# Scores and the second GEMM as 64-row tiles of TensorE in an attention-and-GEMM kernel

## Chip, cores, metric

One core of one Trainium2 chip. The metric is the device time of one execution in microseconds (us), the median of several runs. The engines are named as the profile names them: PE (TensorE matmuls), PEld (its weight loads), DVE (VectorE), ACT (ScalarE), POOL (GpSimd), SP (SyncE, which here only issues transfers).

## The reference, cut to what matters

```python
# q, k, v: (8 batches, 8 heads, 576 tokens, 64); f: (8, 8, 576)
scores = matmul(q, k.T) / 8
scores = where(causal, -1e9, scores + cumsum(log f)[q] - cumsum(log f)[k])
attn   = softmax(scores)
x      = matmul(attn, v)               # -> 4608 tokens x 512
out    = gelu(x @ w_in) @ w_out        # 512 -> 2048 -> 512
```

The kernel works in bf16 with fp32 sums. It folds the forget term into v, so that scores are a bare q k product, then an exponential, a causal mask and AV.

## The kernel before

Batches run one after the other. While batch b is in attention, TensorE fills the gaps of ScalarE's exponentials with the **second GEMM of batch b-1**, one matmul of 128 x 512 a step, 64 steps a batch. Then follows the first GEMM of batch b: 16 tiles of 4 matmuls, each drained by a gelu.

A pair of heads (i, four a batch) has its k transposed in one tile kT of 128 rows: head 0 in rows 0 to 63, head 1 in rows 64 to 127. The contraction of a head is only 64 rows long. The kernel before keeps two copies of q, each with the other head's half zeroed, and runs 128-row matmuls:

```python
qA = [consts.tile([P, S], BF16, ...)]   # head 0 in rows 0-63, zeros below
qB = [consts.tile([P, S], BF16, ...)]   # head 1 in rows 64-127, zeros above

def scores(b, i, t):                    # one of four score tiles of a pair
    on_pe = b == 0 or (b == 1 and i == 0)
    st = s_psum.tile([P, 2, 512], FP32, tag="s")       # two banks; two buffers
    for n, q0, w in STILES[t]:
        for h, qt in enumerate((qA[i], qB[i])):
            nc.tensor.matmul(st[:, h, c : c + w],
                kT[i][:, K0[n] : K0[n] + P], qt[:, q0 : q0 + w], ...)
        if on_pe ...:                   # causal mask, added by TensorE in the first batches
            nc.tensor.matmul(st[:, h, c : c + P], ident_bf, after, start=False, ...)
    nc.scalar.activation(et[:, :, 0:c], st[:, :, 0:c], Act.Exp, scale=scale)
    ...                                 # later batches: mask by GpSimd
```

The second GEMM uses one PSUM bank a block of 128 tokens (16 steps), and one copy to take it out. The same pool `m_psum` (two banks) also serves the first GEMM.

```python
def gemm2(c, ...):                      # a generator: one step a yield
    for ts, kt, ... in order:
        if kt == 0:
            pss[ts] = m_psum.tile([P, d_model], FP32, tag="m")
        nc.tensor.matmul(pss[ts], g_of[c][kt][:, ts * P : (ts + 1) * P],
                         w_out_sb[:, kt, :], start=kt == 0, stop=kt == n_ff - 1)
        if kt == n_ff - 1:
            nc.vector.tensor_copy(ot, pss[ts]); nc.sync.dma_start(out[...], ot)
        yield

FILL = [[4, 6, 2, 2], [2, 2, 2, 2], [2, 2, 2, 2], [2, 2, 1, 1], [8, 0, 20]]
# attention(b): for each pair i and tile t: scores(b, i, t);
#   AV of pair i-1 in parts behind tiles 1, 2 and 3; then FILL[i][t] steps
# last pair: AV, then x by a transposing DMA under 20 more steps (PE transposes for b <= 2)
```

The pools hold eight PSUM banks (PSUM is where this kernel's matmuls write their sums; a bank is counted here as a tile of 128 x 512 fp32): scores 2 x 2, AV (`o_psum`) 2, `m_psum` 2. The change keeps to these eight, so a second bank for a block comes out of one of the three pools.

The softmax here doesn't subtract the row's maximum and nothing guards it: scores larger than these inputs give would overflow.

## Time and profile before

| | before |
|---|---|
| median of the runs | 357.1 us |
| TensorE busy | 346.8 of 356.2 us |
| from the last first-GEMM matmul of one batch to that of the next: batch 1, 2, 3 to 7 | 40.81, 38.14, 37.42 us |

The third row is taken from the trace's single records; the parts before batch 1 vary from run to run by up to a few us; the first GEMM of batch 0 begins at 28.75 here, and the clock record reaches full at 10.7 here. Three rows of the list of groups show the terms (line, engine, operation, out<-in, shapes, count; then busy us and mean ns; then idle time ahead of them and what ended it):

```profile
L308 PE MATMUL s<-qA,kT 128*128 128x256 bf16 (+2 forms) x192 | 51.9, 282 | 2.1 <-ACT e L323 2.0
L323 ACT ACTIVATE e<-s 128x896 bf16<-128x896 f32 (+1 forms) x128 | 105.1, 863 | 19.8 <-PE s L308 11.3
L451 DVE COPY ot<-ps 128x512 f32<-128x512 f32 (+2 forms) x37 | 25.1, 677 | 105.3 <-PE ps L442 105.0
```

Before the score matmuls of this row TensorE stood idle for 2.1 us in the whole span, 2.0 of them for ScalarE, so the schedule has next to no gap. ScalarE needs 0.86 us to drain a scores tile, VectorE 0.68 to take out a block. "128*128" is the part of the array that a matmul uses: this is where a tile of 64 rows will show as 64*128.

### The profile page before, as it was taken

Reading aid. Unit: us, or ns where it says so; the run is one execution under the profiler, and the core shown is the slowest. Engines: PE = TensorE matmul, PEld = TensorE weight load, DVE = VectorE, ACT = ScalarE, POOL = GpSimd, SP = SyncE. Lnnn points to the kernel's source line nnn. Section 1 sums busy time; section 2 is a strip of 40 time slices with the busy share of each in tenths; the row PEclk is TensorE's granted clock in tenths of the full one; section 3 lists DMA queues with packets and bytes.
Section 4 is the critical chain, followed back from the end, with each engine's and each line's share of the span. In section 5 each row is a group of like instructions: output and inputs, shape, how many; then the busy total and the mean of one; then the engine's idle time right before and its main releaser. Section 6 shows DMA issues by size and latency. Waiting matters only on the chain.

```text
span 356.2 us, 7069 instructions
## 1 busy us (share of the span) xinstructions
PE 346.8 (97%) x2756; PEld 190.7 (54%) x2756; DVE 182.1 (51%) x482; ACT 217.4 (61%) x298; POOL 124.5 (35%) x243
## 2 busy tenths in 40 slices
PE   8998989999999999999999999999999999999995
PEld 3784556544664466445654565446544664444443
DVE  6771984595467625781559145924584361011011
ACT  5697586368854797279826882688457854603600
POOL 7390275406546044804470256215520530000000
PEclk9999999999999999999999999999999999999999
DMA  7999999885997894489639973979310132011013
GB/s 116 169 188 191 190 155 202 183 192 90 205 158 161 146 185 122 95 142 189 144 98 134 188 139 82 174 141 173 76 66 2 45 61 81 2 59 59 2 30 88
DMA packets 103936, 43.85 MB, mean 123 GB/s; under 512 B 82720, under 2 KB 99360, under 8 KB 103904
## 3 DMA queue, kind: packets, MB, share of 16 engines
q1 hardware_dynamic: 86608, 29.26, 40.4%
q0 software_dynamic: 16896, 13.63, 25.6%
q10 hardware_dynamic: 400, 0.52, 0.4%
q8 instruction: 21, 0.34, 0.4%
q14 instruction: 11, 0.09, 0.1%
HBM read 36.85 MB, written 9.44 MB: 130 GB/s over the span
## 4 chain that ended last, share of the span: by engine, by line
PE 94%; ACT 2%; DMA 1%; issue 1%; DVE 1%; POOL 0%; ACTq 0%; DVEq 0%; POOLq 0%
PE ps L404 35%; PE ps L442 35%; PE s L308 13%; PE o L344 8%; ACT e L323 2%; PE ps_f L198 1%; DMA k<-in_k_dram 1%; PE s L317 1%; PE ps_w L187 1%; PE ps_x L380 0%; PE s_t L233 0%; PE ps_t L233 0%; DVE x L360 0%; ACT xt L368 0%; ACT g L416 0%
## 5 line engine op out<-in xcount | busy, mean ns | idle before, releaser
L416 ACT ACTIVATE g<-ps 128x512 bf16<-128x512 f32 x144 | 86.0, 597 | 97.9 <-PE ps L404 97.8
L442 PE MATMUL ps<-w_out_sb,g 128*128 128x512 bf16 (+2 forms) x592 | 143.8, 373 | 0.0
L323 ACT ACTIVATE e<-s 128x896 bf16<-128x896 f32 (+1 forms) x128 | 105.1, 863 | 19.8 <-PE s L308 11.3
L404 PE MATMUL ps<-xT,w_in_sb 128*128 128x512 bf16 x512 | 112.9, 379 | 0.7 <-ACT xT L383 0.6
L325 POOL TENSOR_SCALAR_AFFINE_SELECT e<-e 128x256 bf16<-128x256 bf16 x135 | 53.7, 408 | 118.6 <-ACT e L323 117.7
L404 PEld LDWEIGHTS <-w_in_sb 128*128 128x128 bf16 x576 | 56.0, 97 | 69.2 <-issue 3.9
L451 DVE COPY ot<-ps 128x512 f32<-128x512 f32 (+2 forms) x37 | 25.1, 677 | 105.3 <-PE ps L442 105.0
L442 PEld LDWEIGHTS <-g 128*128 128x128 bf16 x592 | 52.2, 98 | 41.8
L292 POOL TENSOR_TENSOR vw<-v_sb,wT 128x640 bf16<-128x640 f32 x32 | 41.0, 1282 | 45.7 <-PE ps_t L233 15.9
L308 PEld LDWEIGHTS <-kT 128*128 128x128 bf16 x384 | 36.7, 98 | 33.3 <-issue 6.2
L308 PE MATMUL s<-qA,kT 128*128 128x256 bf16 (+2 forms) x192 | 51.9, 282 | 2.1 <-ACT e L323 2.0
L308 PE MATMUL s<-qB,kT 128*128 128x256 bf16 (+2 forms) x192 | 48.6, 282 | 0.0
L344 PE MATMUL o<-vw,e 128*128 128x65 bf16 x960 | 43.5, 194 | 0.5 <-ACT e L323 0.4
L344 PEld LDWEIGHTS <-e 128*128 128x128 bf16 x960 | 39.5, 98 | 7.5 <-ACT e L323 0.5
L359 DVE RECIPROCAL r<-o 128x5 f32<-128x5 f32 x64 | 12.5, 195 | 41.5 <-PE o L344 41.0
L276 DVE COPY kT<-tk 64x288 bf16<-64x288 bf16 x96 | 32.3, 336 | 1.4
L360 DVE TENSOR_TENSOR x<-o,r 128x256 bf16<-128x256 f32 x64 | 27.2, 425 | 2.4 <-DVE r L359 0.2
L276 DVE COPY qB<-tq 64x288 bf16<-64x288 bf16 x48 | 18.8, 391 | 0.6
L370 DVE TENSOR_SCALAR xt<-o,r 64x64 bf16<-64x64 f32 x60 | 17.5, 291 | 1.4
L276 DVE COPY qA<-tq 64x288 bf16<-64x288 bf16 x48 | 17.1, 355 | 1.1
L404 PE MATMUL ps<-tails,w_in_sb 128*128 128x512 bf16 x64 | 14.4, 377 | 0.0
L416 ACT ACT_TABLE_LOAD x8 | 10.3, 1283 | 0.1
(63 smaller groups left out, 124.4 us busy)
## 6 DMA issues: line engine op xcount, KB each, us to landing
out_dram<-ot SPq DMA_DIRECT2D x32, 256.0 KB, 2.2
v_sb<-in_v_dram SPq DMA_DIRECT2D x20, 256.0 KB, 4.7
v_sb<-in_v_dram SPq DMA_DIRECT2D x29, 128.0 KB, 5.4
q<-in_q_dram POOLq DMA_DIRECT2D x6, 576.0 KB, 6.6
k<-in_k_dram POOLq DMA_DIRECT2D x6, 576.0 KB, 9.0
w_in_sb<-in_moe_w_in_dram POOLq DMA_DIRECT2D x4, 512.0 KB, 7.6
w_out_sb<-in_moe_w_out_dram POOLq DMA_DIRECT2D x4, 512.0 KB, 9.6
q<-in_q_dram POOLq DMA_DIRECT2D x4, 144.0 KB, 4.1
```

The costliest lines, as they stand in the source:

```text
L276: nc.vector.tensor_copy(rows[:, odd], src[odd * D : (odd + 1) * D, 2 * i + h].rearrange("d j p -> d p j"),)
L292: nc.gpsimd.tensor_tensor(vw_of[b][:, hs, :, 0:D], v_sb[:, hs, :, :], w.unsqueeze(3).to_broadcast([P, 2, NBLK, D]), Alu.mult,)
L308: nc.tensor.matmul(st[:, h, c : c + w], kT[i][:, K0[n] : K0[n] + P], qt[:, q0 : q0 + w], start=True, stop=not on_pe or c not in SDIAG[t],)
L323: nc.scalar.activation(et[:, :, 0:c], st[:, :, 0:c], Act.Exp, scale=scale)
L325: nc.gpsimd.affine_select(out=et[:, :, c0 : c0 + P], in_=et[:, :, c0 : c0 + P], compare_op=Alu.is_ge, fill=0.0, base=0, pattern=[[0, 2], [ ...
L344: nc.tensor.matmul(o[:, m, :], e_of[b, i, t][:, h, c : c + P], vw_of[b][:, 2 * i + h, n, :], start=(n == 0), stop=(n == m),)
L360: nc.vector.tensor_tensor(x_of[b, i][:, :, h, :], o[:, 0:4, 0:D], r[:, 0:4].unsqueeze(2).to_broadcast([P, NBLK - 1, D]), Alu.mult,)
L370: nc.vector.tensor_scalar(*tail, r[D:P, 4:5], None, Alu.mult)
L404: nc.tensor.matmul(ps, w_in_sb[:, kt, ffb * P : (ffb + 1) * P], src[:, kt, :], start=(kt == 0), stop=(kt == n_dm - 1),)
L416: nc.scalar.activation(g_of[c][ffb], ps, Act.Gelu)
L442: nc.tensor.matmul(pss[ts][:, c0:c1], g_of[c][kt][:, ts * P : (ts + 1) * P], w_out_sb[:, kt, c0:c1], start=(kt == 0), stop=(kt == n_ff - 1),)
L451: nc.vector.tensor_copy(ot[:, c0:c1], pss[ts][:, c0:c1])
```

## The change

Its intent: run the two heads' score matmuls at the same time as two tiles of 64 rows, with no zeros (qT replaces qA and qB). A change between tilings takes 0.09 us in the trace of the kernel before (from 13.06 to 13.15, between 128*128 and 96*64), so the second GEMM's steps that stand among the scores are made of 64-row tiles too: each step is two half contractions into two banks, added on the way out by a copy and an add. AV stays at 128 rows, so it moves into one stretch a pair, with some whole steps ("n") between its two heads.

```diff
-            for h, qt in enumerate((qA[i], qB[i])):
+            for h in range(2):
+                d = slice(h * D, (h + 1) * D)
                 nc.tensor.matmul(
                     st[:, h, c : c + w],
-                    kT[i][:, K0[n] : K0[n] + P],
-                    qt[:, q0 : q0 + w],
+                    kT[i][d, K0[n] : K0[n] + P],
+                    qT[i][d, q0 : q0 + w],
...
+    STEPS = [16 * "r", "rrrnnrrrrrrrrnnn", "rrrrrrrrrrnnrrrr", 8 * "r" + 8 * "n"]
+    def gemm2_rows(c):
+        for ts, steps in enumerate(STEPS):
+            if ts < n_sub - 1:
+                banks = [m_psum.tile([P, d_model], FP32, tag="m", name="ps2")
+                         for _ in range(2)]
+            else:
+                both = s_psum.tile([P, 2, d_model], FP32, tag="s", name="ps2")
+                banks = [both[:, 0], both[:, 1]]
+            for kt, step in enumerate(steps):
+                last = kt == steps.rindex("r")
+                for r in range(2 if step == "r" else 1):
+                    rows = slice(r * D, (r + 1) * D) if step == "r" else slice(0, P)
+                    nc.tensor.matmul(banks[r], g_of[c][kt][rows, ...],
+                                     w_out_sb[rows, kt, :], ...)
+                if last:
+                    nc.vector.tensor_copy(ot, banks[1])
+                if kt == n_ff - 1:
+                    nc.vector.tensor_tensor(ot, ot, banks[0], Alu.add)
...
-    FILL = [[4, 6, 2, 2], [2, 2, 2, 2], [2, 2, 2, 2], [2, 2, 1, 1], [8, 0, 20]]
+    FILL = [[6, 6, 4, 0], [0, 3, 2, 2], [2, 2, 3, 3], [2, 2, 2, 2], [8]]
+    FILL_AV = [2, 3, 2, 2]
+    def attention(b):                     # batches 2 to 7
+        def av(i):
+            for h in range(2):
+                attend(b, i, h, (0, 1, 2, 3, 4)); normalize(b, i, h)
+                if h == 0: take(fill, FILL_AV[i])
+        # per pair: tiles 0 and 1, av(i - 1), tiles 2 and 3, with FILL steps between
+        take(fill, FILL[HP][0]); av(HP - 1); take(fill, 6)
+        to_xT(b, HP - 1, nc.vector.tensor_copy, o_psum, "o")
```

Batches 0 and 1 get the tiled scores too, but keep their order: in batch 1 the second GEMM stays whole. In batch 0 and the first pair of batch 1 the 128-row mask matmuls stay among the scores.

More of the change, by code (lines that the diff above doesn't have):

```diff
@@ L142 @@
     make_identity(nc, ident_fp)
-    qA = [consts.tile([P, S], BF16, name=f"qA{i}") for i in range(HP)]
-    qB = [consts.tile([P, S], BF16, name=f"qB{i}") for i in range(HP)]
+    qT = [consts.tile([P, S], BF16, name=f"qT{i}") for i in range(HP)]
     kT = [consts.tile([P, S], BF16, name=f"kT{i}") for i in range(HP)]
-    def zero_halves(pairs):
-        for i in pairs:
-            nc.vector.memset(qA[i][D:P, :], 0.0)
-            nc.vector.memset(qB[i][0:D, :], 0.0)
     w_in_sb = consts.tile([P, n_dm, d_ff], BF16)
@@ L174 @@
     nc.vector.memset(ones, 1.0)
-    zero_halves(range(2))
     nc.vector.memset(wT[0:D, 4, :], 0.0)
@@ L202, in transposes_first @@
                 )
-        def evac(eng, dst, r0, r1):
-            op = eng.copy if eng is nc.scalar else eng.tensor_copy
-            op(
-                dst[r0:r1, :].rearrange("d (p j) -> d p j", j=JT),
-                ps[r0:r1].rearrange("d j p -> d p j"),
-            )
-        if which:
-            evac(nc.vector, kT[i], 0, P)
-        else:
-            evac(nc.vector if i else nc.scalar, qA[i], 0, D)
-            evac(nc.vector, qB[i], D, P)
+        op = nc.scalar.copy if i == 0 and not which else nc.vector.tensor_copy
+        op(
+            (qT, kT)[which][i].rearrange("d (p j) -> d p j", j=JT),
+            ps.rearrange("d j p -> d p j"),
+        )
     def transposes_pe(b, i, pool):
@@ L239, in transposes_pe @@
             for h in range(2):
-                dst = (qA[i], qB[i])[h] if which == 0 else kT[i]
+                dst = (qT, kT)[which][i]
                 rows = dst[h * D : (h + 1) * D, :].rearrange(
@@ L270, in untangle @@
             for h in range(2):
-                dst = (qA[i], qB[i])[h] if which == 0 else kT[i]
+                dst = (qT, kT)[which][i]
                 rows = dst[h * D : (h + 1) * D, :].rearrange(
@@ L461, in gemm2 @@
             yield
+    STEPS = [16 * "r", "rrrnnrrrrrrrrnnn", "rrrrrrrrrrnnrrrr", 8 * "r" + 8 * "n"]
+    def gemm2_rows(c):
+        for ts, steps in enumerate(STEPS):
+            if ts < n_sub - 1:
+                banks = [
+                    m_psum.tile([P, d_model], FP32, tag="m", name="ps2")
+                    for _ in range(2)
+                ]
+            else:
+                both = s_psum.tile([P, 2, d_model], FP32, tag="s", name="ps2")
+                banks = [both[:, 0], both[:, 1]]
+            ot = o_pool.tile([P, d_model], FP32, tag="ot", name="ot")
+            for kt, step in enumerate(steps):
+                last = kt == steps.rindex("r")
+                for r in range(2 if step == "r" else 1):
+                    rows = slice(r * D, (r + 1) * D) if step == "r" else slice(0, P)
+                    nc.tensor.matmul(
+                        banks[r],
+                        g_of[c][kt][rows, ts * P : (ts + 1) * P],
+                        w_out_sb[rows, kt, :],
+                        start=(kt == 0),
+                        stop=last if r else kt == n_ff - 1,
+                    )
+                if last:
+                    nc.vector.tensor_copy(ot, banks[1])
+                if kt == n_ff - 1:
+                    nc.vector.tensor_tensor(ot, ot, banks[0], Alu.add)
+                    nc.sync.dma_start(
+                        out[c * S + ts * P : c * S + (ts + 1) * P, :], ot
+                    )
+                yield
     def take(gen, n):
@@ L481, in first_attention @@
         transposes(0, o_psum, "o")
-        zero_halves(range(2, HP))
         warm_up(4)
@@ L534, in first_attention, with second_attention @@
         to_xT(0, 3, nc.vector.tensor_copy)
-    FILL = [[4, 6, 2, 2], [2, 2, 2, 2], [2, 2, 2, 2], [2, 2, 1, 1], [8, 0, 20]]
+    FILL = [[6, 6, 4, 0], [0, 3, 2, 2], [2, 2, 3, 3], [2, 2, 2, 2], [8]]
+    FILL_AV = [2, 3, 2, 2]
     FILL_1 = [[0, 4, 4, 0], [0, 2, 3, 3], [4, 4, 4, 4], [3, 3, 3, 3], [8, 0, 99]]
-    def attention(b, fill, counts):
+    def attention(b):
+        fill = gemm2_rows(b - 1)
+        def av(i):
+            for h in range(2):
+                attend(b, i, h, (0, 1, 2, 3, 4))
+                normalize(b, i, h)
+                if h == 0:
+                    take(fill, FILL_AV[i])
+        for i in range(HP):
+            for t in range(4):
+                scores(b, i, t)
+                take(fill, FILL[i][t])
+                if i and t == 1:
+                    av(i - 1)
+                    if i < HP - 1 or b > 2:
+                        x_dma(b, i - 1)
+                if t == 1 and i == 0:
+                    load_v(b + 1)
+                if b > 2 and t == 0 and i < 2:
+                    transpose_dma(b + 1, 4 * i, 4 * i + 4)
+                if b == 2 and t == 1 and i == 1:
+                    transpose_dma(3, 0, 4)
+                    transpose_dma(3, 4, 8)
+        take(fill, FILL[HP][0])
+        if b == 2:
+            to_xT(b, HP - 2, nc.vector.tensor_copy, o_psum, "o")
+        av(HP - 1)
+        take(fill, 6)
+        to_xT(b, HP - 1, nc.vector.tensor_copy, o_psum, "o")
+        x_tail_dma(b)
+        take(fill, 999)
+    def second_attention():
+        b, fill, counts = 1, gemm2(0, True), FILL_1
         for i in range(HP):
@@ L552, in attention @@
                     normalize(b, i - 1, 1)
-                    if i < HP - 1 or b > 2:
+                    if i < HP - 1:
                         x_dma(b, i - 1)
-                if t == 1 and i == 0 and b > 1:
-                    load_v(b + 1)
-                if b > 2 and t == 0 and i < 2:
-                    transpose_dma(b + 1, 4 * i, 4 * i + 4)
-                if b == 2 and t == 3 and i == 1:
-                    transpose_dma(3, 0, 4)
-                    transpose_dma(3, 4, 8)
-                if b == 1 and (i, t) == (0, 2):
+                if (i, t) == (0, 2):
                     transposes_pe(1, 3, o_psum)
-                if b == 1 and i == 1 and t in (0, 2):
+                if i == 1 and t in (0, 2):
                     weigh_v(1, 2 + t // 2)
-                if b == 1 and t == 3:
+                if t == 3:
                     if i == 1:
@@ L573, in attention @@
         take(fill, counts[HP][0])
-        if b <= 2:
-            to_xT(b, i - 1, nc.vector.tensor_copy, o_psum, "o")
+        to_xT(b, i - 1, nc.vector.tensor_copy, o_psum, "o")
         attend(b, i, 0, (0, 1, 2, 3, 4))
@@ L580, in attention @@
         normalize(b, i, 1)
-        if b <= 2:
-            take(fill, 7)
-            to_xT(b, i, nc.vector.tensor_copy, o_psum, "o")
-        else:
-            x_dma(b, i)
+        take(fill, 7)
+        to_xT(b, i, nc.vector.tensor_copy, o_psum, "o")
         x_tail_dma(b)
-        if b == 1:
-            transpose_dma(2, 4, 8)
-            load_v(2, 4, 8)
+        transpose_dma(2, 4, 8)
+        load_v(2, 4, 8)
         take(fill, 999)
@@ L594 @@
             first_attention()
+        elif b == 1:
+            second_attention()
         else:
-            attention(b, gemm2(b - 1, b == 1), FILL_1 if b == 1 else FILL)
+            attention(b)
         if b == 0:
```

## The prediction

> **What bounds the kernel now.** I read the page first, then the chain of work that ended last, in order of time, then the timeline of one middle batch. The page:
>
> ```profile
> PE 346.8 (97%) x2756; PEld 190.7 (54%) x2756; DVE 182.1 (51%) x482; ACT 217.4 (61%) x298; POOL 124.5 (35%) x243
> ...
> PE ps L404 35%; PE ps L442 35%; PE s L308 13%; PE o L344 8%; ACT e L323 2%; PE ps_f L198 1%; DMA k<-in_k_dram 1%; PE s L317 1%; PE ps_w L187 1%; PE ps_x L380 0%; PE s_t L233 0%; PE ps_t L233 0%; DVE x L360 0%; ACT xt L368 0%; ACT g L416 0%
> ```
>
> TensorE is the bound: the chain lies on it for 94% of the span. Scores (L308) hold 13% of it, some 46 us, and their moving operand is half zeros (qA, qB), so half of that is waste: 23 us is the ceiling of the change. The chain in order of time (start, length, what) gives the period:
>
> ```profile
> 37.38 0.51 PE s_t L233 x12
> ...
> 177.13 1.94 PE ps L442 x9
> 179.07 0.95 PE o L344 x30
> 180.02 4.32 PE ps L442 x20
> 184.34 13.89 PE ps L404 x64
> ...
> 221.76 13.89 PE ps L404 x64
> ```
>
> Batches 3 to 7 repeat every 221.76 - 184.34 = 37.42 us. 13.89 / 64 = 0.217 us is one 512-column matmul, so the 64 of the second GEMM take 13.85; AV takes 0.95 per 30, 3.81 for 120; the rest, 37.42 - 13.89 - 13.85 - 3.81 = 5.87, is scores plus 0.26 of waits. Before, there is nearly no wait to win back. The timeline (start, length, engine, line, operation), PE alone at the start, then all engines in a middle batch:
>
> ```profile
> 12.95 0.27 PE L317 MATMUL s<-after,ident_bf 128*128 128x128 bf16 x2
> 13.15 0.47 PE L198 MATMUL ps_f<-ident_bf,k 96*64 96x96 bf16 x10
> ...
> 13.52 0.45 PE L198 MATMUL ps_f<-ident_bf,q 96*64 96x96 bf16 x10
> 13.90 0.28 PE L308 MATMUL s<-qA,kT 128*128 128x256 bf16 x1
> ...
> 160.43 0.38 PE L404 MATMUL ps<-xT,w_in_sb 128*128 128x512 bf16 x1
> ...
> 161.46 1.28 ACT L323 ACT_TABLE_LOAD   x1
> ...
> 162.76 4.17 ACT L323 ACTIVATE e<-s 128x896 bf16<-128x896 f32 x5
> 163.73 0.35 PE L308 MATMUL s<-qA,kT 128*128 128x448 bf16 x1
> ...
> 165.64 0.24 PE L308 MATMUL s<-qB,kT 128*128 128x192 bf16 x1
> 165.72 0.59 PE L442 MATMUL ps<-w_out_sb,g 128*128 128x512 bf16 x2
> ...
> 166.36 0.69 DVE L451 COPY ot<-ps 128x512 f32<-128x512 f32 x1 [7.02 <-PE ps L442]
> ```
>
> What the reader is to see: (a) The transposes L198 are already tiles of 64 columns (96*64). The second L317 starts at 13.01 and streams 0.055, to 13.06, yet L198 begins at 13.15; the last L198 (0.21 long) starts at 13.76, streams 0.04, and L308 begins at 13.90. **A change of tiling costs 0.09 us**, in either direction. (b) ScalarE starts its exponentials at 162.76, 2.1 us after the last matmul of the first GEMM streamed out (160.65): the last gelu and a table load of 1.28 lie between. The first five take 4.17, the last of them 0.92, so they start 0.81 apart (behind the short fourth tile of a pair I count 0.6); the fifth starts at 166.01, 0.29 after its scores streamed out (165.64 + 0.08). The third scores tile starts at 163.73 because it needs the first one's PSUM buffer: free 0.97 after the exponential began. (c) The evacuation L451 starts 0.20 after the last second-GEMM matmul streamed out (166.16) and takes 0.69.
>
> [...] the trace has column tiles only: 24 transposes took about 0.65 us (13.15 to 13.80) where 12 of L233 in 128-column form, with the same 96 columns, took 0.51, so two tiles run at once: 24 / 0.65 is 1.6 times 12 / 0.51, with the change of tiling's ramp still in it. No run yet shows it for rows. [...]
>
> **The change part by part.**
> Scores: a pair of heads has 1664 columns per head. From the starts, 192, 256, 320, 448 and 128 columns take 0.082, 0.109, 0.136, 0.188 and 0.056, so a pair costs 2 x 0.707 = 1.41 and a batch 5.66. With two row tiles at once half goes: **-2.83 a batch**.
> Second GEMM: a row step is two half matmuls at once over the same 512 columns, 0.216 as before: 0. It is tiled only so that TensorE does not change tiling between scores and the filling among them.
> Tiling changes, batches 2 to 7: in and out of AV for pairs 0 to 2 (6), into rows at the start, out for the last AV: 8 x 0.093 = **+0.75**.
> The last pair's x goes by TensorE again (4 transposes of 0.055, **+0.22**) in place of the transposing DMA; its second-GEMM cover of 20 matmuls is spent earlier.
> VectorE: 4 more operations of 0.69 a batch, 2.8 on some 20 of 37: not the bound, but TensorE now needs *both* m buffers for a block, so it waits for the add.
> Waits, worked through a batch (s12 is pair 1's scores tile 2, a block is one 128-token output block of the second GEMM, 16 steps) from t = 0 at the end of the first GEMM, with scores 0.192, 0.192, 0.189, 0.136 per tile, 0.216 a step, 0.477 a head of AV; a scores buffer comes free 0.97 after its exponential starts, an exponential starts 0.29 after its scores streamed out or 0.81 behind the last one:
> - s00 0.09 to 0.29, 6 steps to 1.58, s01, 6 steps to 3.07, s02 (exponential 0 began 2.11, free 3.08) to 3.28, 4 steps to 4.14: block 0 is full. s03 to 4.28. s10 needs exponential 2 (began 3.73): 4.70, waits **0.42**. s11 needs the one of 4.57 (0.7 long): 5.33, waits **0.43**.
> - Block 1 needs the add of block 0: 4.14 + 0.20 + 2 x 0.70 + 0.05 = 5.79; s11 ended 5.52, waits **0.27**. Before stood at 5.89 here with the same 16 steps and the same tiles done: until here ScalarE sets the pace, and all that faster scores gain is 0.1.
> - 3 steps, change, AV 0 with 2 steps, change, 8.01. s12 to 8.20, its exponential at 8.49, free 9.46; s20 could start 9.20, waits **0.26**.
> - Block 1 ends inside AV 1 at 11.93. Its add stands on VectorE behind the first half's normalization (to 12.59), ends 13.28; block 2 could start 12.68, starts 13.33, waits **0.65**.
> - Block 3 takes a scores buffer: its exponential began 18.04, free 19.00, ready 18.75, waits **0.25**.
> - End: last step 23.51, transposes to 23.73; VectorE does block 3's add (23.71 to 24.40) ahead of the xT copy (0.43): the fourth matmul of the first GEMM waits from 24.38 to 24.88, **0.50**.
> Sum of waits 2.78, against 0.26 of the same sort and 0.08 at the first GEMM before: +2.44. A batch: -2.83 + 0.75 + 0.22 + 2.44 = +0.6. Batch 2 had the transposes before: +0.4. Six batches: 5 x 0.6 + 0.4 = +3.4.
> Batch 0: masks stay 128-row matmuls between scores: 5 stretches a pair, 40 changes, of which 4 were there already: 36 x 0.093 = 3.3 against -2.83, **+0.5**. The 8 zero fills (0.3 each) and 4 VectorE copies (0.75) that go free no end: the first scores wait for the warm-up matmuls anyway. Batch 1: the first pair waits for ScalarE (1.15 and 0.63 of gaps), which absorbs its part; pairs 1 to 3 gain 2.1 and pay 22 changes, 2.0: **0**. Sum: 357.2 + 3.4 + 0.5 = 361; I go down to **360**, since every wait was rounded to the late side and tuned numbers like these fills speak for a schedule that fits better than my walk.
>
> **Rivals.** (1) *The scores' saving arrives*: had the schedule no new waits, a batch would be 2.83 - 0.75 - 0.22 = 1.9 shorter, 11.3 in six, near 346. For it: fills were chosen around buffers. Against it: ScalarE's 2.1 us of late start and the add on VectorE lie in program order. (2) *Row tiles overlap badly*: each of 49 row steps and 24 score groups a batch costs 0.02 more: 1.5 a batch, near 369. Against it: the column tiles. (3) *A change costs more with rows than with columns*, say 0.15: 48 + 36 + 22 = 106 new changes by 0.06 more, 6 us, near 366. The single-precision transposes (64*128) at 11.6 show about 0.09 each way too, which speaks against it.
>
> **Range and chances.** Waits too high by half would give 353; a mild form of rival 2 or 3, 366. 353 to 366 holds it 8 times in 10. Faster by over 2% (under 350.0) needs rival 1 nearly whole: 0.08. Slower by over 2% (over 364.3): 0.14. Within 2%: 0.78.
>
> **What would show it.** The start-to-start of successive first GEMMs at 38.0 in place of 37.42; pairs of 64*128 score matmuls starting nearly together, 0.70 per pair of heads; gaps of 0.09 at each change; waits of PE on ScalarE at the second pair's first tiles, and on VectorE's adds for block 2 and for xT. Wrong if row steps take over 0.22, if the changes are hidden, or if the period falls under 36.5.

## The result

| | before | after |
|---|---|---|
| median of the runs | 357.08 us | 365.22 us |
| span of the profiled execution | 356.2 us | 363.2 us |
| TensorE busy | 346.8 us | 343.2 us |
| batch 1, 2, 3 to 7 | 40.81, 38.14, 37.42 us | 41.34, 38.80, 38.80 us |

**2.3% slower**: the ratio is 1.0234 (95% interval 1.0213 to 1.0255). Here and below a ratio is the mean time of one kernel's fast runs over that of the other's fast runs of the same rounds, so it is not quite the ratio of the medians quoted.

The page of the changed kernel, busy times and the chain that ended last:

```profile
PE 343.2 (94%) x3028; PEld 176.4 (49%) x3070; DVE 204.2 (56%) x499; ACT 216.8 (60%) x298; POOL 124.7 (34%) x243
...
PE 78%; ACT 9%; DVE 7%; issue 3%; DMA 1%; POOL 1%; ACTq 0%; POOLq 0%
```

The chain lay on TensorE for 94% before and does for 78% now; ScalarE and VectorE have 16% of it. That is the signature of a schedule that was tight and is not any more: 3.6 us less of busy TensorE, 7 us more of span. The chain in order of time, for the end of one batch and the begin of the next:

```profile
180.81 0.93 ACT e L311
181.78 1.92 PE ps L473 x16
183.72 0.70 DVE ot L481
...
187.94 4.91 PE ps L392 x22
...
226.74 4.91 PE ps L392 x22
```

From 187.94 to 226.74 is 38.80, where it was 37.42. Pieces of VectorE (L481 is the copy of one half, L483 the add) and of ScalarE (L311) now stand between TensorE's. The timeline of TensorE shows each gap, with what ended it in brackets:

```profile
162.40 0.37 PE L296 MATMUL s<-qT,kT 64*128 64x256 bf16 x4
162.60 0.38 PE L473 MATMUL ps<-w_out_sb,g 64*128 64x512 bf16 x1
163.16 1.45 PE L473 MATMUL ps<-w_out_sb,g 64*128 64x512 bf16 x11 [0.18 <-ACT g L404]
...
165.93 0.38 PE L473 MATMUL ps<-w_out_sb,g 64*128 64x512 bf16 x1
165.93 0.35 PE L296 MATMUL s<-qT,kT 64*128 64x448 bf16 x1
...
168.13 0.37 PE L296 MATMUL s<-qT,kT 64*128 64x320 bf16 x4 [0.42 <-ACT e L311]
...
173.12 0.61 PE L473 MATMUL ps<-w_out_sb,g 64*128 64x512 bf16 x4
173.66 0.65 PE L332 MATMUL o<-vw,e 128*128 128x65 bf16 x15
...
176.09 0.80 PE L473 MATMUL ps<-w_out_sb,g 64*128 64x512 bf16 x5 [0.16 <-DVE ot L483]
...
184.47 0.38 PE L473 MATMUL ps<-w_out_sb,g 128*128 128x512 bf16 x1 [0.20 <-DVE ot L481]
...
187.94 2.32 PE L392 MATMUL ps<-xT,w_in_sb 128*128 128x512 bf16 x10 [0.24 <-DVE xT L371]
```

The same place in the kernel before, from the first score matmul of a batch to the first step behind it:

```profile
160.65 0.27 PE L308 MATMUL s<-qA,kT 128*128 128x256 bf16 x1
...
161.03 1.03 PE L442 MATMUL ps<-w_out_sb,g 128*128 128x512 bf16 x4
```

Read from the top. Four score matmuls now take 0.20 (162.40 to 162.60) where they took 0.38 (160.65 to 161.03), so **the tiles do what was hoped of them**. Then the first half matmul of the second GEMM starts at 162.60 and its partner only at 163.16: it waited for "ACT g", a gelu. At 165.93 a second-GEMM matmul starts (165.926) just before the second half of the scores (165.934) that stands ahead of it in the program: here the two row tiles run as separate streams, and the first one (rows 0 to 63) is one matmul ahead. At 168.13 scores wait for an exponential, at 176.09 a half matmul waits for an add, at 184.47 a whole step waits for a copy, at 187.94 the first GEMM waits for xT. The last of the four half matmuls at 173.12 starts 0.61 - 0.38 later and holds the array for 0.22 (the distance at which such matmuls follow each other): 173.57. AV starts at 173.66, so one change of tiling took 0.09.

Where do the 7.2 us between the two profiled executions come from, counted to the end of batch 7's first GEMM? Batches 3 to 7 give 5 x 1.38 = 6.9, batch 2 0.67, batch 1 0.53, and the stretch to the end of batch 0's first GEMM gives -0.92. The last is no gain of the change: TensorE's clock rose to full at 10.7 us in the execution of before and at 6.5 in the one after, by the trace's clock records (until then 512-column matmuls stand 0.427 apart, thereafter 0.216). An experiment below that has batch 0 exactly as before began its first GEMM at 27.47, the changed kernel at 27.84; the experiments with the changed kernel's batch 0 began it at 27.3 to 28.3, so a smaller difference than that can't be read from single executions.

### The profile page after: what moved, and what is told of

Same layout as the page of the kernel before. It is cut to its first block, busy times and chain, and to the rows that moved or that the text cites. A ratio compares the mean times of both kernels' runs of the same rounds, so it can differ in the third digit from the quotient of the medians.

```text
span 363.2 us, 7651 instructions
## 1 busy us (share of the span) xinstructions
PE 343.2 (94%) x3028; PEld 176.4 (49%) x3070; DVE 204.2 (56%) x499; ACT 216.8 (60%) x298; POOL 124.7 (34%) x243
## 4 chain that ended last, share of the span: by engine, by line
PE 78%; ACT 9%; DVE 7%; issue 3%; DMA 1%; POOL 1%; ACTq 0%; POOLq 0%
PE ps L392 33%; PE ps L473 19%; PE ps L430 11%; ACT e L311 7%; PE o L332 7%; PE s L296 5%; DVE ot L483 2%; DVE ot L481 2%; DMA k<-in_k_dram 1%; ACT g L404 1%; PE s L305 1%; DVE x L348 1%; DVE xT L371 1%; PE ps_f L192 1%; DVE xt L358 0%
## 5 line engine op out<-in xcount | busy, mean ns | idle before, releaser
L311 ACT ACTIVATE e<-s 128x896 bf16<-128x896 f32 (+1 forms) x128 | 104.6, 862 | 38.9 <-PE s L296 33.4
L473 PE MATMUL ps<-w_out_sb,g 64*128 64x512 bf16 (+1 forms) x654 | 104.1, 376 | 4.4 <-ACT g L404 1.0
L473 PEld LDWEIGHTS <-g 64*128 64x128 bf16 (+1 forms) x678 | 41.1, 94 | 34.4 <-issue 12.2
L296 PE MATMUL s<-qT,kT 64*128 64x320 bf16 (+4 forms) x384 | 52.5, 281 | 5.5 <-ACT e L311 4.5
L263 DVE COPY qT<-tq 64x288 bf16<-64x288 bf16 x96 | 46.6, 485 | 1.5
L430 PE MATMUL ps<-w_out_sb,g 128*128 128x512 bf16 (+2 forms) x200 | 43.4, 362 | 0.4
L481 DVE COPY ot<-ps 128x512 f32<-128x512 f32 x24 | 16.6, 692 | 41.2 <-PE ps L473 41.2
L439 DVE COPY ot<-ps 128x512 f32<-128x512 f32 (+2 forms) x13 | 8.4, 650 | 50.0 <-PE ps L430 49.9
L296 PEld LDWEIGHTS <-kT 64*128 64x128 bf16 x384 | 21.4, 94 | 29.1 <-issue 18.6
L430 PEld LDWEIGHTS <-g 128*128 128x128 bf16 x208 | 18.8, 98 | 18.9 <-issue 0.4
L483 DVE TENSOR_TENSOR ot<-ot,ps 128x512 f32<-128x512 f32 x24 | 16.5, 688 | 2.4 <-PE ps L473 1.8
```

Source lines behind the costliest of these rows:

```text
L263: nc.vector.tensor_copy(rows[:, odd], src[odd * D : (odd + 1) * D, 2 * i + h].rearrange("d j p -> d p j"),)
L296: nc.tensor.matmul(st[:, h, c : c + w], kT[i][d, K0[n] : K0[n] + P], qT[i][d, q0 : q0 + w], start=True, stop=not on_pe or c not in SDIAG[t],)
L430: nc.tensor.matmul(pss[ts][:, c0:c1], g_of[c][kt][:, ts * P : (ts + 1) * P], w_out_sb[:, kt, c0:c1], start=(kt == 0), stop=(kt == n_ff - 1),)
L473: nc.tensor.matmul(banks[r], g_of[c][kt][rows, ts * P : (ts + 1) * P], w_out_sb[rows, kt, :], start=(kt == 0), stop=last if r else kt == n ...
L481: nc.vector.tensor_copy(ot, banks[1])
```

## The experiments

All gave the right result. "Batch" is the period of batches 3 to 7 in the profiled execution, which repeats within 0.02 us but for the odd pause; the medians also contain the uneven start.

| run | median us | ratio to before | batch us |
|---|---|---|---|
| before | 357.1 to 357.9 | 1 | 37.42 |
| the change | 365.22 | 1.0234 | 38.80 |
| e1_n_after_heads | 364.51 | 1.0184 | 38.44 |
| e2_half_in_o | 362.46 | 1.0166 | 38.27 |
| e3_xT_before_add | 362.29 | 1.0161 | 38.40 |
| e5_three_waits (e1, e2, e3) | 358.16 | 1.0034 | 37.50 |
| e10_add_before_norm (e5 and one more) | 356.44 | 0.9974 | 37.15 |
| e7_order_alone | 362.70 | 1.0155 | 38.43 |
| e4_scores_alone | 359.75 | 1.0070 | 37.76 |
| e6_bursts | 355.40 | 0.9927 | 36.50 |
| e8_bursts_all | 354.03 | 0.9903 | 36.50 |
| e9_bursts_x_first | 353.79 | 0.9875 | 36.50 |
| e11_first_batch_kept | 351.47 | 0.9837 | 36.50 |

My theory after the result: the walk through a batch in the prediction was right, but left out two waits that the timeline shows, the one at 163.16 and the one at 184.47. The main rival: those waits cost nothing, since ScalarE, which starts its exponentials 2.1 us after TensorE's last first-GEMM matmul, sets the pace anyway. The first three kernels take one wait away each; then all three go together.

### The whole steps behind both heads

```diff
-    FILL_AV = [2, 3, 2, 2]
+    FILL_AV = [2, 3, 2, 0]
...
-        take(fill, 6)
+        take(fill, 8)
```

> The two whole steps of block 3 stand behind both heads of the last AV, not between them. My theory: in the changed kernel the first of them waited 0.36 us, not for its data but because the copy of the other half stands in the same two-bank tile, and the order of accesses is kept by tile. Here the copy has 2 x 0.477 + 0.09 = 1.05 us instead of 0.57, and it needs 0.20 + 0.69 + 0.05 = 0.94, so the wait goes: the batch period falls from 38.80 to 38.44, the time from 365.2 to about 363.0 (ratio to before 1.017). Rival: the wait is for VectorE in general (its normalizations), then it only moves to the next step: period 38.7 or more, 364.6 or more.

The period is 38.44, to the digit. TensorE's timeline of one batch's end:

```profile
185.50 1.12 PE L332 MATMUL o<-vw,e 128*128 128x65 bf16 x30
186.47 1.89 PE L473 MATMUL ps<-w_out_sb,g 128*128 128x512 bf16 x8
188.19 0.39 PE L368 MATMUL ps_x<-ident_bf,x 128*128 128x128 bf16 x4
```

AV's 30 matmuls and then the eight whole steps follow without a break. The step that waited did not read what the copy reads: it adds to bank 0 of a two-bank tile while VectorE copies bank 1. The program orders accesses by tile, so it waited all the same. The traces have a control for this. Block 1 has its halves in two tiles, and there, in the next experiment, VectorE copied one half from 172.40 to 173.09 while whole steps into the other started at 172.78 and 173.00, right behind AV and without a wait.

The median fell by only 0.7, not 2.2. In the profiled execution a load of v landed 0.5 us later in batch 0 than in the changed kernel, the granted clock was half for 3.4 us while the first GEMM ran, and the first GEMM of batch 1 began 1.9 us later. That is the slowest of the four runs, though; the others were granted 0.999 to 1.0 of the clock and have no trace, so what held them is not shown. The best had 363.4, near the 363.0 expected.

### The second half of block 0 in another pool

```diff
-                banks = [m_psum.tile(...) for _ in range(2)]
+                pools = [(m_psum, "m"), (m_psum, "m")]
+                if ts == 0:
+                    pools[1] = o_psum, "o"
+                banks = [pool.tile([P, d_model], FP32, tag=tag, name="ps2")
+                         for pool, tag in pools]
```

> Block 0 keeps its second half in a bank of the AV pool, which is idle then, in place of the second m buffer. My theory: in the changed kernel the first second-half matmul of a batch waited 0.34 us because the second m buffer still held the last tile of the first GEMM, until its gelu ended; the delay, and the 0.2 us by which the second half's stream then lagged, went on to the exponentials and the blocks behind (0.48 us later than I had walked by block 3). Here the wait goes: the period falls by 0.34 to 0.5, to 38.3 to 38.46, the time to 362.2 to 363.2. Rival: ScalarE's late start (2.1 us) sets the pace of the first two pairs, so the wait costs nothing: period 38.7 or more, time 364.6 or more.

The period is 38.27, 0.53 less, just over the expected 0.34 to 0.5. TensorE's timeline at the start of a batch:

```profile
161.57 0.37 PE L296 MATMUL s<-qT,kT 64*128 64x256 bf16 x4
161.77 1.46 PE L476 MATMUL ps<-w_out_sb,g 64*128 64x512 bf16 x12
163.06 0.35 PE L296 MATMUL s<-qT,kT 64*128 64x320 bf16 x4
```

Six steps stand in one piece, and the scores behind them in one piece too: the two streams go side by side. In the changed kernel the second stream lagged by one matmul, 0.2 us, and an exponential needs both halves of its scores tile. So the 0.34 of the wait itself came back as 0.53, and the rival is out as it stood. ScalarE's late start does set its first two exponentials, which begin 2.32 and 3.14 after the start of the last first-GEMM matmul in both kernels; but the third waited for its scores and began at 4.29, against 3.93 here, where the first six follow each other without a gap (4.80 us). From the third on, the wait for the m buffer was on the path.

### xT ahead of the add

```diff
-        take(fill, 6)
+        take(fill, 5)
         to_xT(b, HP - 1, nc.vector.tensor_copy, o_psum, "o")
         x_tail_dma(b)
         take(fill, 999)
```

> The last pair's transposes stand before the last step of block 3, so that VectorE copies xT ahead of block 3's add. My theory: the 0.41 us wait of the first GEMM's fourth matmul is VectorE's program order (add, 0.69, then copy, 0.42). The period falls by 0.4 to 38.4, the time to about 362.8. Rival: it waits for the normalization of the last head, which would then hold the transposes up instead: no change, 365.

The period is 38.40 and the median 362.29, both as expected. The transposes now stand ahead of the last step and the first GEMM runs on without a break:

```profile
185.12 0.39 PE L368 MATMUL ps_x<-ident_bf,x 128*128 128x128 bf16 x4
185.35 0.38 PE L473 MATMUL ps<-w_out_sb,g 128*128 128x512 bf16 x1
185.56 2.75 PE L392 MATMUL ps<-xT,w_in_sb 128*128 128x512 bf16 x12
```

### The three together

Its edit is the sum of the three (the last with 7 steps for 8).

> The three edits of the first three experiments together. My theory: the three waits lie one after the other on TensorE's path, so they add: 38.80 - 0.36 - 0.53 - 0.40 = 37.5 a batch, time about 357.5, ratio to before 1.00: what is left of the loss of the change is then nothing, and of the gain nothing either. Rival: with one wait gone another takes its place (scores buffers, block 2's add), so they do not add: period 37.9 or more, time 359.7 or more.

The waits add: 38.80 - 0.36 - 0.53 - 0.40 = 37.51, measured 37.50. Two pieces of its chain, one batch apart, each within the first GEMM:

```profile
184.59 8.42 PE ps L392 x39
...
222.10 8.42 PE ps L392 x39
```

222.10 - 184.59 = 37.51. What is left is the time of the kernel before, with 2.8 us of TensorE work a batch on zeros taken out and nothing to show for it.

### The add ahead of a normalization

On top of the three: block 1 ends between the heads of AV 1, and VectorE did the first head's normalization before its add.

```diff
                 attend(b, i, h, (0, 1, 2, 3, 4))
+                if h == 0 and i == 1:
+                    take(fill, FILL_AV[i])
                 normalize(b, i, h)
-                if h == 0:
+                if h == 0 and i != 1:
                     take(fill, FILL_AV[i])
```

> The changed kernel without its three waits (37.50 a batch), and in AV of pair 1 the add of block 1 stands on VectorE ahead of the first head's normalization. Tests the one large wait that the prediction listed and no run has touched: block 2 waits 0.65 us for that add because of VectorE's program order. Theory: the add ends 0.45 us or more earlier, the period falls from 37.50 to about 37.05, time from 358.2 to 355.5. Rival: the scores buffers pace the stretch and take the time back: 37.3 or more, 357 or more.

The period fell to 37.15, by 0.35 where 0.45 was expected; the median is 356.44. So this wait of the prediction's list was real and on the path too, with a small part taken back elsewhere. 356.44 over before is 0.9974, interval 0.9941 to 1.0007: not clearly faster than the kernel before.

### The order alone

The kernel before with the changed order (fill counts, AV stretches, the last x by TensorE) but no tiles and no second bank.

```diff
+        fill = gemm2(b - 1)            # whole steps, one bank a block
         # attention(b) otherwise as in the changed kernel; scores with qA and qB
```

> The kernel before in the order of the changed one (fill counts, AV in one stretch, x of the last pair by TensorE), nothing tiled, one bank a block. It tells the cost of the order from that of the tiles. My walk: waits of 0.12, 0.55, 0.13 at the scores buffers and 0.49 at xT in place of 0.34 before, and 0.22 of transposes: 37.42 + 0.95 + 0.22 = 38.6, so nearly all of the changed kernel's +1.38 would be its order, while the tiles' saving and their own costs cancel. Rival: the order is harmless alone (37.5 to 37.8) and the loss comes with the second bank.

The period is 38.43. The order alone, without any tile, costs **1.01** of the 1.38 us a batch, 0.22 of it for the transposes of the last x. TensorE's timeline shows its largest wait for a scores buffer, where the fill counts leave nothing to do between three score tiles:

```profile
166.52 0.24 PE L308 MATMUL s<-qA,kT 128*128 128x192 bf16 x1
166.60 0.24 PE L308 MATMUL s<-qB,kT 128*128 128x192 bf16 x1
167.22 0.30 PE L308 MATMUL s<-qA,kT 128*128 128x320 bf16 x1 [0.38 <-ACT e L323]
```

A matmul of 192 columns holds the array for 0.08 (166.60 - 166.52), so the scores end at 166.68; the next start at 167.22: 0.54. The tiles then add 0.37 net: 2.83 saved, and more than that spent. Both kernels wait at some of the same places (for ScalarE at pair 1's scores, for xT), so neither number is the cost of a part that one could subtract from any other version.

### The scores alone

The kernel before, with qT and row-tiled scores; order and second GEMM as before.

```diff
-            for h, qt in enumerate((qA[i], qB[i])):
+            for h in range(2):
+                d = slice(h * D, (h + 1) * D)
```

> The kernel before with the scores as 64-row tiles and nothing else: the second GEMM whole, the order as before. Theory: half of the scores goes (-2.83 a batch), and each of the 16 score tiles of a batch costs a change of tiling in and out, 32 x 0.095 = 3.0, the waits for ScalarE at the start stay: period 37.5 to 37.7, time 358.5 to 360. Rival (a change costs less where TensorE goes on at once, or is hidden in the waits): period 36.5 or less, time under 354.

The period is 37.76, just over the range of 37.5 to 37.7. In one batch of its trace I count 31 gaps of 0.09 to 0.11 us at a change of tiling, 3.0 together, against 2.83 saved; the remaining 0.17 was not followed up. So the reason given for tiling the second GEMM is right: tiles for the scores alone are eaten by the changes. In batch 1, which has this very form in the changed kernel too, the period is 41.34 in both, 0.53 over before.

### Scores in bursts

If 16 changes of tiling a batch are had for 1.54, one needs neither a split second GEMM nor its adds. The scores pool holds two tiles: issue two, change, do second-GEMM steps and one head of AV at 128 rows, change back.

```diff
+    FILL = [[15, 6], [5, 6], [5, 6], [5, 5], [3, 7]]
+    def bursts(b):                      # batches 2 to 7
+        fill = gemm2(b - 1)
+        for i in range(HP):
+            for u in range(2):
+                scores(b, i, 2 * u); scores(b, i, 2 * u + 1)
+                take(fill, FILL[i][u])
+                if i: av(i - 1, u)      # one head: attend and normalize
+        take(fill, 3); av(HP - 1, 0); av(HP - 1, 1); take(fill, 7)
+        to_xT(b, HP - 1, ...); take(fill, 999)
```

> The scores as 64-row tiles in bursts of two score tiles (the pool's two buffers), then a change of tiling, second GEMM whole (one bank a block, no adds) and one head of AV, then a change back: 16 changes of 0.096 = 1.54 a batch in place of the changed kernel's 8, but no split second GEMM, no add, no second m buffer. Theory: what the change paid for sparing 8 changes (0.77) were waits worth more. From the kernel before: -2.83 + 1.54 + 0.22 (the last pair's transposes) - 0.3 (waits) = -1.3 to -1.0: period 36.1 to 36.4, time 350 to 352. Rival: both tiles of a burst must be drained by ScalarE before the next (2.26 us from burst to burst against some 2.3 of work), so ScalarE paces it: period 37 or more, 355 or more.

The period is 36.50, 0.1 above the expected range and far from the rival's 37: bursts beat the kernel before by 0.92 a batch and the change by 2.30. No run has the order of the bursts without tiles. The kernel before had 0.34 of waits a batch (as the prediction counts them), so by an estimate the order alone could give no more than that, and the tiles give at least 0.58 of the 0.92. One round of TensorE's timeline:

```profile
169.60 0.50 PE L296 MATMUL s<-qT,kT 64*128 64x448 bf16 x4
170.03 1.47 PE L430 MATMUL ps<-w_out_sb,g 128*128 128x512 bf16 x6
171.34 0.64 PE L332 MATMUL o<-vw,e 128*128 128x65 bf16 x15
171.91 0.56 PE L296 MATMUL s<-qT,kT 64*128 64x256 bf16 x8
```

Scores, six steps, a head of AV, scores again: 2.31 us a round, with no bracket, that is no wait. The median, 355.40, is over the expected 350 to 352. In the profiled execution (355.87) the transposed x of pair 1 landed late in batch 2 (at 109.9), behind four other transfers of the same queue, and TensorE waited 2.4 us for it. After that pause its matmuls ran at half pace for about 3.4 us; batch 2 took 40.98, and batch 5 had another pause for an x (37.24). The other three runs (353.52 to 356.1) were granted the full clock, so the half pace is not what all of them lost.

### Bursts in all batches, and the queue's order

Two edits in turn. The first moved batches 0 and 1 to bursts, with their mask matmuls behind the rows of a burst. The second moved, in batch 2, the four transfers of q and k behind that of x.

```diff
-                if b == 2 and u == 1 and i == 1:
+                if b == 2 and u == 1 and i == 2:
                     transpose_dma(3, 0, 4)
                     transpose_dma(3, 4, 8)
```

> As the bursts, and also in batches 0 and 1: scores of two tiles in a burst where they stand together, and the mask matmuls (128 rows) behind the rows of the burst and not among them, so that they pay no change of their own. Batch 0 then has some 20 changes for 36, batch 1 16 for 32: 1.5 and 1.5 less at most, part of it hidden in waits for ScalarE. Time 1 to 2.5 us under the bursts alone, 348 to 350, ratio to before under 0.98. Rival: batches 0 and 1 are paced by ScalarE and the loads: within 0.5 us of the bursts alone.

> The bursts in all batches, with one edit: in batch 2 the four transposing transfers of q and k stand behind the transfer of x of pair 1 on the queue, not ahead of it. In the two burst kernels that x landed at 109.9 and 111.2, 2.1 to 2.3 us after TensorE had begun the first GEMM of batch 2, which waited for it. Theory: that wait goes, batch 2's period falls from 39.1 to 36.7 to 37.0, time from 354.0 to 351 to 352, the other batches stay at 36.50. Rival: the q and k of batch 3 then come late for VectorE's copies and hold up batch 3 by as much: 353.5 or more.

The first: 354.03, ratio 0.9903. Batch 1's period fell from 41.34 to 39.94, but the first GEMM of batch 0 began 1.5 us later than in e6 and, with the clock at half for 3.4 us, ended 3.0 later, and batch 2 still took 39.10, so the expected ratio under 0.98 was missed. The second: batch 2's period fell to 37.15, 0.15 above the expected range, yet the median stayed at 353.79 (351.43 to 354.98), where 351 to 352 was expected. Its profiled execution waited 2.2 us for k's early load, the clock fell to a half for 3.4 us, and the first GEMM began at 31.1 (27.3 in e6). The miss lies in batch 0 and not where the edit was.

The last kernel keeps the second edit and the bursts of batch 1, and gives batch 0 back its order of the change.

> The bursts in batches 1 to 7 with x of pair 1 first, and batch 0 as in the changed kernel (masks among the rows, one score tile at a time). In the two kernels with batch 0's masks moved, TensorE waited for early loads, its granted clock fell to a half for 3.4 us in the profiled runs, and the runs spread over 1.8 to 3.5 us; the batches 3 to 7 stayed at 36.50. Theory: batch 0's shorter path gains nothing, since the loads set it[...]: median 351.5 to 353 with batch periods unchanged. Rival: the spread comes from the loads alone, whatever the order: median 353.5 to 354.5 as the last kernel.

351.47, ratio **0.9837** (0.9796 to 0.9877): the best of all, 1.6% faster than the kernel before. Its median is at the lower end of the theory's range, but one of its six runs had 355.83, so the uneven start is rarer at most. The clock is not cured either: in the profiled execution (352.44) it was at half from 48.30 to 51.71, now in batch 1, and batch 1 took 41.54 for e9's 39.93. Whether batch 0's order caused the uneven start or the loads of those runs is not settled. Its page:

```profile
PE 335.8 (96%) x2733; PEld 173.3 (49%) x2776; DVE 186.2 (53%) x475; ACT 216.1 (62%) x298; POOL 125.2 (36%) x243
...
PE 89%; POOL 2%; issue 2%; DMA 2%; ACT 2%; DVE 1%; SPq 1%; POOLq 0%; ACTq 0%
```

TensorE's busy time is 11 us under the kernel before, and the chain lies on it for 89%.

## Why the prediction was wrong

It said 360 and gave "slower by over 2%" a chance of 0.14; 365.2 is within its range, but the change of time is three times the one forecast (8.1 for 2.8). Step by step:

- **Scores, -2.83 a batch**: right. A group of four took 0.20 for 0.38.
- **A row step costs what a whole one does**: right; within one stream they stand 0.215 to 0.216 apart. Rival 2, that row tiles overlap badly, is out.
- **A change costs 0.09**: right, 0.09 to 0.11 at full clock wherever it was counted (the changed kernel, e4, e6), for rows as for columns (0.09 to 0.10 between 128*128 and 96*64 in the kernel before). Rival 3 is out.
- **"Waits, worked through a batch"**: this step failed. Each wait in the list was there: in order, 0.22, 0.58, 0.31, 0.23, 0.54, 0.23 and 0.41 were measured for 0.42, 0.43, 0.27, 0.26, 0.65, 0.25 and 0.50. The walk ended at 38.02, the trace at 38.80. Two waits were *not* in the list. First, a batch's first row step needs both m buffers, and the second still holds the last tile of the first GEMM until its gelu ends: with the lag that it leaves between the two streams it costs 0.53 (e2). The walk had asked what block 1 waits for and not what block 0 does. With this wait gone the walk holds nearly to the digit: in e2 pair 1's first two score tiles start at 4.70 and 5.29 after the first GEMM (walked: 4.70 and 5.33), pair 2's first at 9.47 (9.46), block 2 at 13.26 (13.33). Second, block 3's whole steps share a two-bank tile with the half that is being copied out: 0.36 (e1). Together 0.89, less the 0.09 by which xT's was too high: 0.80, against the 0.78 that was missing. (A slip without effect: the prediction's 5.87 is scores plus 0.21, not 0.26; the trace's two waits for scores buffers do add up to 0.26.)
- **Batches 0 to 2**: batch 2 +0.67 for +0.4, batch 1 +0.53 for 0. Batch 1's first pair was to absorb its changes of tiling in its waits for ScalarE, but those stayed as long as before (0.96 and 0.55 for 0.99 and 0.47 in the two profiles); no run tested it further. Batch 0 was forecast at +0.5; with the clock apart it is near 0.4 by the single comparison above, and its sign is within the spread.
- **"I go down to 360"**: the wrong way. The walk gave 361, and its waits were not too long but too few. With 0.78 more in five batches, 0.27 in batch 2 and 0.53 in batch 1 it would have been 365.7, or 365.2 with no loss in batch 0.
- **Rival 1**, that the saving arrives: it did not with this schedule. e5 and e10 show by how much each wait kept it back, and the bursts that about 0.9 of the 2.83 can be had a batch, once the waits are gone and 1.54 is paid for changes and 0.22 for transposes.

So the question that a large change with a small effect leaves, where the gain went, has this answer: half matmuls take TensorE 0.20 us for 0.38 in a group of four scores, but at the first six score tiles ScalarE sets the pace (in e2 its exponentials run there without a gap, 4.80 us), and the second bank and the add, which were the price for sparing eight changes of tiling (0.77 us), made TensorE wait for longer than that: 0.53, 0.36 and 0.35 by e2, e1 and e10. The order that this needed was not free by itself either (e7).

## What to carry to other kernels

When a tightly packed engine is given less work, ask which other engine each buffer waits for *before* counting the saving; here the two waits that were missed follow, once seen, from the order of the program. A second accumulator per block doubles the buffers held at the moment a block begins, so also walk through who held the second one last. And measure a switching cost before building around it: at 0.09 us a change of tiling is cheaper here than one wait for a copy (0.36), and a schedule with 16 changes a batch did better than one with 8.

## What the traces show of tilings and of the clock

- A change of tiling, at full clock: 0.09 to 0.11 us each way between 128*128 and 64*128 (31 such gaps in one batch of e4), 0.09 to 0.10 between 128*128 and 96*64 in the kernel before.
- In the changed kernel the order of starts was not always that of the program: at 165.93 a second-GEMM matmul of the first row tile (rows 0 to 63) started (165.926) before the scores' second half (165.934) that stands ahead of it. The two halves of the first scores of a batch started 3 to 4 ns apart (162.403 and 162.406, 162.522 and 162.526).
- In a run of row steps of the changed kernel, 512-column half matmuls of one row tile stood 0.215 to 0.216 us apart, as whole ones do, with a weight load (94 ns) of the same rows for each: the loads added nothing to that distance.
- A matmul waited for the copy of another bank of the same two-bank tile; that is the program's way of keeping order, and cost 0.36 us a batch (e1).
- The granted clock fell to a half for 3.41 us at a time in the profiled executions of e1, e6, e8, e9 and e11. What came before it differed: a single wait of 2.4 us in e6, one of 2.2 in e9, while in e1, e8 and e11 the profile shows no wait over 0.61, 0.61 and 1.37 us in the 9 us before it. What sets it off no run shows.
